# Attention with a top-1 expert mixture on one core: a mask in another pool, two reordered steps, one PSUM bank and new order edges at the changeover

## The chip, the core and the metric

The kernel runs on one core of one Trainium2 chip. The metric is the device time of one execution in microseconds (us); three executions of the kernel before lie between 932.32 and 932.95 us, their median is 932.58 us.

## The reference, cut to what matters

```python
# attention: B=8 batches, H=8 heads, S=576 positions, D=64
scores = q @ k^T / 8 + min(-(cum_i - cum_j), 0)      # cum = cumsum(max(s, 0)); above the diagonal: -1e9
attn   = softmax(scores); x = (attn @ v) as 4608 tokens of 512 values
# mixture: 4 groups of 4 experts, one expert for each token
g_logits = x @ w_group;     g = argmax;  g_w = softmax(g_logits)[g]
e_logits = x @ w_expert[g]; e = argmax;  e_w = softmax(e_logits)[e]
out[token] = g_w * e_w * (relu(x @ w1[g, e]) @ w2[g, e])     # w1: 512 x 1024, w2: 1024 x 512
```

## The kernel before, in words

**Two stages.** Attention runs head by head (64 steps, two heads are a pair `p`), and the mixture runs expert by expert (16 "slots", the fullest expert first). Every product is made of two or three matmuls on high and low parts of its operands, so that each float32 operand is first cast (ScalarE, `wh`, `xh`, `hh`) and its rest is formed by a subtraction (GpSimd or VectorE, `wl`, `xl`, `hl`).

**The order in attention.** `ORDERS` and `FIRST` (L484 to L493) are strings that say in which order the pieces of a step are issued on TensorE, VectorE, ScalarE and GpSimd; these engines work in just this order. `A0` to `A5` are matmuls of a head's row maxima into two PSUM banks `pm` (A1: 64 columns, A2: 192, A3: 320, A4: 448, A5: the second 288), `a` is the maximum that VectorE takes over the oldest of them (`most`, `mx`), `W` is a transpose of `st` on VectorE, `B` and `C` are the scores and the products with V, and `R` runs the next piece of the router. A matmul `A` needs a `pm` bank that an `a` has read. Score tiles, transposes and the router's logits take their banks from `ring`, three banks `ps`; the router's later sums share one bank `pt` (`kept`).

**The router.** For each batch of 576 tokens `Router.batch` is a generator that `R` steps on. Its pieces, in order: the logits (`logits`, L683: 512 columns and the last 64, copied to `lT` by ScalarE), the transposes `pr` of the last 64 rows, the turning matmuls `plt` (L765) with the maximum `lmx` over them (L774), the one-hot choice (`hot`), the counts `pc` (L802), the places in the lists, `rows` and `val`, the list sums `pi` and `pw` (L862), and the weights (`weights`, `finish`; ScalarE's copy `c3p`, L899, ahead of three products `val`, of which the first runs on GpSimd for all batches but the last, L906).

**The changeover.** From step 62 on only TensorE keeps a written order; the other engines' instructions are ordered by a planner that runs the program in its own model and takes what is ready there. The first slot's work is traced after the attention, and `behind(tc, later, earlier)` adds an edge to the order alone: `later` stands behind `earlier`. The first slot has 256 rows of the fullest expert as its `h_items` (96 matmuls `ph`, list `made`, L1383) and `y_items` (64 of `first`, then 32 of `last`, matmuls `py`), and a `rest` tile of 128 more rows, whose token list needs the last batch's list sums. Expert 0's weights come in four loads of 1 MB (`raw`, L1000): two for w1, two for w2; each is cast in four pieces (`wts[0].casts[0]` to `[15]`, L1002, ScalarE) and has four subtractions (`wl`, L1005, GpSimd). The first `py` needs casts from `[8]` on, the `last` matmuls need `wl`.

**Memory.** The pools of attention lie one behind the other in SBUF: `raw` (27648 bytes of each partition), `wa` (77824), `big` (22528), `sm` (15808), `late`, `end`. Those of the mixture use the same bytes again from the same start: `x1` (28672), `wp` (65536), `hp` (24576), `x2` (26624: `xg1`, the third load `raw`, `xh`, `xl`), `wq`, `sp`. A tile waits for the tiles whose bytes it takes.

Of the kernel before, what the change touches and what calls it, by code (L numbers as in the profile page):

```python
# [8 lines left out]
F32 = mybir.dt.float32  # L9
# [3 lines left out]
AF = mybir.ActivationFunctionType  # L13
# [6 lines left out]
B, H, S, D = 8, 8, 576, 64  # L20
P = 128
# [84 lines left out]
def behind(tc, later, earlier):  # L106

    tc.add_manual_dep(later.ins, earlier.ins.name, mybir.DependencyInfo(mybir.DependencyClass.NoSync,
                                                                       mybir.DependencyReason.DATA), reason="behind")


def attention(tc, qk, v, s, wr, xs, st):
    nc = tc.nc
    NP = B * H // 2
    LEAD = 4
    with ExitStack() as ctx:
# [4 lines left out]
        sm = ctx.enter_context(tc.tile_pool(name="sm", bufs=2))  # L121
        late = ctx.enter_context(tc.tile_pool(name="late", bufs=1))
        end = ctx.enter_context(tc.tile_pool(name="end", bufs=1))
        ac = late
# [318 lines left out]
        ones(2)  # L443
        ones(1)

        mask = ac.tile([P, S], F32, name="mask")
        nc.gpsimd.memset(mask, 0.0)
        nc.gpsimd.affine_select(out=mask[:, S - P:], in_=mask[:, S - P:], pattern=[[-1, P]],
                                compare_op=ALU.is_ge, fill=-8.0e9, base=0, channel_multiplier=1)
# [24 lines left out]
        def store_sums():  # L474
# [7 lines left out]
        vals, sums, pts = {}, {}, {}  # L482

        ORDERS = [o.split() for i, o in enumerate((  # L484
# [16 lines left out]
        for step in [-4, -3] + list(range(NH + 5)):  # L501
            m, a = step + LEAD, step - 1
# [109 lines left out]
class Router:  # L612
# [70 lines left out]
    def logits(self, b, x):  # L683

        nc, lT = self.tc.nc, self.lT
        out = []
        for a, e in ((0, 512), (512, S)):
            ps = self.ps_s(f"lg{b}_{a}")
            for c in range(4):
                i = nc.tensor.matmul(ps[32 * c:32 * c + 32, 0:e - a], self.wr_f[:, c], x[:, c, a:e], start=True, stop=True)  # L690
            out.append((lT[:, a:e], ps[:, 0:e - a]))
        for o, ps in out:
            nc.scalar.copy(o, ps)  # L693
        self.st.logged = i
# [37 lines left out]
    def batch(self, b, x):  # L732
        tc, sm, st = self.tc, self.sm, self.st
        nc = tc.nc
# [15 lines left out]
        ps = self.ps_s(f"pr{b}")  # L750
# [12 lines left out]
        ps = self.ps_t(f"plt{b}")  # L763
        for t in range(NB):
            st.turned = nc.tensor.matmul(ps[:, t * 20:(t + 1) * 20], lT[:, t * P:(t + 1) * P], self.sum4,  # L765
                                         start=(t == 0), stop=(t == NB - 1))
        G = [P, NB * 5, 4]

        def quads(c):
# [8 lines left out]
        df = T("df", G[1:])  # L778
        V.tensor_tensor(out=df, in0=lgv, in1=mb, op=ALU.subtract)
        ex = df  # L780
# [67 lines left out]
        C4 = [P, NB, E * NL]  # L848
# [21 lines left out]

        def weights(bank):
            if b != B - 2:
                nc.scalar.activation(ex, df, AF.Exp)
                yield 1
            wf = bank[:, 128:128 + NB * 5]
            w = wf.rearrange("p (t g) -> p t g", g=5)
            cwp, rem = bank[:, 160:160 + NB], bank[:, 168:168 + NB]
            c3p = bank[:, 176:176 + 3 * NB].rearrange("p (j t) -> p j t", t=NB)
            with after(tc, st.routed):
                summed = V.tensor_reduce(out=wf, in_=ex, axis=AX.X, op=ALU.add)  # L880
            if b == B - 2:
                st.put_off.append(summed)
            V.tensor_scalar(out=wf, in0=wf, scalar1=1e-9, scalar2=None, op0=ALU.add)
            V.reciprocal(wf, wf)
            yield
            ws = T("ws", [NB, 4])
            V.tensor_tensor(out=ws, in0=w[:, :, 1:5], in1=oh[:, :, 0], op=ALU.mult)
            wsum = T("wsum", [NB])
            V.tensor_reduce(out=wsum, in_=ws, axis=AX.X, op=ALU.add)
            for x in (cwp, st.cw[:, b]):  # L890
                V.tensor_tensor(out=x, in0=wsum, in1=w[:, :, 0], op=ALU.mult)
            yield

            c3 = T("c3", [3, NB], BF16)
            V.tensor_copy(c3[:, 0], cwp)
            V.tensor_tensor(out=rem, in0=cwp, in1=c3[:, 0], op=ALU.subtract)
            V.tensor_copy(c3[:, 1], rem)
            V.tensor_tensor(out=c3[:, 2], in0=rem, in1=c3[:, 1], op=ALU.subtract)
            nc.scalar.copy(c3p, c3)  # L899
            return c3, c3p  # L900

        def finish(c3, c3p):
            for j in range(3):
                yield
                with after(tc, st.routed):
                    if b < B - 1 and j == 0:  # L906
                        nc.gpsimd.tensor_tensor(out=val[:, 2 + j], in0=colf, in1=c3[:, j].unsqueeze(2).to_broadcast(C4),
                                                op=ALU.mult)
                    else:
                        st.valued = V.tensor_tensor(out=val[:, 2 + j], in0=colf,  # L910
                                                    in1=c3p[:, j].unsqueeze(2).to_broadcast(C4), op=ALU.mult)
            yield 2
            listed(2, 5, "pw")
# [22 lines left out]
def moe(tc, w1, w2, xs, st, out):  # L936
    nc = tc.nc
    V = nc.vector
    ident, mc = st.ident, st.cst
    with ExitStack() as ctx:  # L940
# [93 lines left out]
        class Slot:  # L1034


            def __init__(self, u, w, cap, xg, ids, cw):
                self.u, self.w, self.cap, self.xg, self.ids, self.cw = u, w, cap, xg, ids, cw
                self.rows = [min(P, cap - t) for t in range(0, cap, P)]
                self.products, self.turns, self.highs = [], [], []  # L1040

            def gather(self):
                for t, r in enumerate(self.rows):
# [40 lines left out]
            def h_items(self):  # L1084
                u, cap = self.u, self.cap
                self.hh = hp.tile([P, 8, 384], F32R, name=f"hh{u}", tag="hh")
                self.hl = hp.tile([P, 8, 384], F32R, name=f"hl{u}", tag="hl")

                pss = {}

                def first(f):

                    pss[f] = acc(f"ph{u}_{f}")
                    half(f, 0)
                    half(f, 2)

                def half(f, c0):
                    for c in (c0, c0 + 1):
                        for x in (self.xh, self.xl):
                            product(f, self.w.h, x, c)  # L1100

                def opening():
                    for f in range(4):
                        pss[f] = acc(f"ph{u}_{f}")
                    for c in (0, 2):
                        for f in (1, 2, 0, 3):
                            half(f, c)

                def last(f):
                    for c in range(4):  # L1110
                        product(f, self.w.l, self.xh, c)
                    relu(f)

                def relu(f):
                    ps, hh = pss.pop(f), self.hh[:, f, :cap]
                    self.rounded = nc.scalar.activation(hh, ps[:, :cap], AF.Relu)  # L1116
                    V.scalar_tensor_tensor(out=self.hl[:, f, :cap], in0=ps[:, :cap], scalar=0.0,  # L1117
                                           in1=hh.bitcast(F32), op0=ALU.max, op1=ALU.subtract)

                def product(f, w, x, c, stop=None):  # L1120
                    self.products.append(nc.tensor.matmul(pss[f][:, :cap], w[f // 4][:, c, (f % 4) * P:(f % 4 + 1) * P], x[:, c, :cap],  # L1121
                                     start=(c == 0 and w is self.w.h and x is self.xh),
                                     stop=(c == 3 and w is self.w.l) if stop is None else stop))

                def item(f):
                    if f == 0:

                        pss[f] = acc(f"ph{u}_{f}")
                        for c0 in (0, 2):
                            for w in (self.w.h, self.w.l):  # L1130
                                for c in (c0, c0 + 1):
                                    product(f, w, self.xh, c, False)
                        for c in range(4):
                            product(f, self.w.h, self.xl, c, c == 3)
                        relu(f)
                        return
                    first(f)
                    last(f)

                if u == 0:  # L1140

                    return [opening] + [lambda f=f, part=part: part(f) for part, h in ((last, 0), (first, 4), (last, 4))
                                        for f in range(h, h + 4)]
                return [lambda f=f: item(f) for f in range(8)]
# [169 lines left out]
        wts = [Expert(0, st.e0[0:1, 0:1]), Expert(1, st.e0[0:1, 1:2])]  # L1314
# [56 lines left out]
        with tc.manual_schedule(engines={ENG.PE}):  # L1371
# [10 lines left out]
            run(h)  # L1382
            made = first.products  # L1383
            behind(tc, made[34], st.logged)
            behind(tc, made[45], st.turned)
            behind(tc, made[63], st.counted)
            Y, R = first.y_items(), rest.items()
            del made[:]
            run(Y[:5])
            behind(tc, made[3], st.listed[0])  # L1390
            behind(tc, st.listed[2], made[-4])
            run(Y[5:6])
            run(R[:1])
# [269 lines left out]
```

## Time and profile before

| | |
|---|---|
| median of three executions | 932.58 us |
| the profiled execution, its span | 931.89 us, 930.1 us |
| TensorE busy (share of the span) | 870.8 us (94%) |
| VectorE, ScalarE, GpSimd busy | 690.0, 609.7, 620.1 us (74%, 66%, 67%) |
| mean granted TensorE clock | 0.974 of 2.4 GHz |

The profile is one execution. A line of the timeline has the start in us, the busy time in us, the engine, the source line, the operation, what it writes and reads, how many instructions are merged in the line, and in brackets how long the engine sat idle just before and whose result ended that. PE is TensorE, DVE VectorE, ACT ScalarE, POOL GpSimd, SP the queue that issues the loads. PEclk is the granted TensorE clock (1.00 is 2.4 GHz, 0.50 is 1.2 GHz).

### The profile page before, as it was taken

Reading aid. Unit: us, or ns where it says so; the run is one execution under the profiler, and the core shown is the slowest. Engines: PE = TensorE matmul, PEld = TensorE weight load, DVE = VectorE, ACT = ScalarE, POOL = GpSimd, SP = SyncE. Lnnn points to the kernel's source line nnn. Section 1 sums busy time; section 2 is a strip of 40 time slices with the busy share of each in tenths; the row PEclk is TensorE's granted clock in tenths of the full one; section 3 lists DMA queues with packets and bytes.
Section 4 is the critical chain, followed back from the end, with each engine's and each line's share of the span. In section 5 each row is a group of like instructions: output and inputs, shape, how many; then the busy total and the mean of one; then the engine's idle time right before and its main releaser. Section 6 shows DMA issues by size and latency. Waiting matters only on the chain. (4 is left out here: it accounts for less than half of the span.)

```text
span 930.1 us, 17673 instructions
## 1 busy us (share of the span) xinstructions
PE 870.8 (94%) x5689; PEld 788.6 (85%) x5689; DVE 690.0 (74%) x1986; ACT 609.7 (66%) x1310; POOL 620.1 (67%) x732
## 2 busy tenths in 40 slices
PE   4999999999999999999879999999999999999993
PEld 3788787888878787887768999999999999999992
DVE  7677585858768585885548578898888898888830
ACT  3688686777767777766537467657676666766740
POOL 8798475666757575643467756666777778878750
PEclk9999999999999999999879999999999999999997
DMA  7776565465546555423525645446554556655510
GB/s 151 179 169 177 128 161 141 123 162 144 154 99 161 142 144 139 109 84 138 187 82 194 214 162 198 184 167 227 177 205 170 210 175 226 228 208 196 185 44 23
DMA packets 65004, 148.10 MB, mean 159 GB/s; under 512 B 7588, under 2 KB 40996, under 8 KB 54728
## 3 DMA queue, kind: packets, MB, share of 16 engines
q1 hardware_dynamic: 55020, 126.98, 45.6%
q0 software_dynamic: 7488, 18.89, 5.6%
q10 hardware_dynamic: 2396, 1.02, 0.4%
q8 instruction: 47, 0.77, 0.4%
q14 instruction: 53, 0.43, 0.2%
HBM read 108.97 MB, written 19.69 MB: 138 GB/s over the span
## 5 line engine op out<-in xcount | busy, mean ns | idle before, releaser
L1005 POOL TENSOR_TENSOR wl<-raw,wh 128x512 fp32r<-128x512 f32 x182 | 232.3, 1297 | 47.8 <-ACT wh L1002 34.7
L159 POOL TENSOR_TENSOR WB<-r,WA 64x576 fp32r<-64x576 f32 x128 | 181.5, 1418 | 32.9 <-PE pm L208 7.1
L216 DVE CUSTOM_DVE_ANT_0 mx<-pm,mask 128x192 bf16<-128x192 f32 (+4 forms) x320 | 128.9, 418 | 44.4 <-PE pm L208 41.7
L1002 ACT CAST wh<-raw 128x512 fp32r<-128x512 f32 x256 | 153.9, 617 | 0.4 <-POOL wl L1005 0.4
L208 PE MATMUL pm<-WA 66*128 66x288 f32 (+4 forms) x384 | 129.6, 363 | 22.0 <-DVE mc L216 10.5
L1121 PE MATMUL ph<-xh,wh 128*128 128x256 f32 (+13 forms) x512 | 142.7, 305 | 2.6 <-ACT xh L1078 1.9
L1121 PE MATMUL ph<-xl,wh 128*128 128x256 f32 (+13 forms) x512 | 139.7, 304 | 0.3
L265 PE MATMUL ps<-WA 68*128 68x320 f32 (+4 forms) x384 | 136.7, 360 | 3.2 <-ACT lT L693 2.2
L284 POOL TENSOR_SCALAR_AFFINE_SELECT pt<-pt 128x128 f32<-128x128 f32 (+2 forms) x192 | 64.1, 338 | 96.8 <-ACT pt L275 92.3
L1191 PE MATMUL py<-hh,wh 128*128 128x256 f32 (+13 forms) x448 | 116.0, 307 | 6.3 <-ACT wh L1002 6.3
L305 PE MATMUL po<-pt,VT 128*128 128x256 f32 (+3 forms) x512 | 120.4, 355 | 0.4 <-issue 0.3
L1191 PE MATMUL py<-hl,wh 128*128 128x256 f32 (+13 forms) x448 | 117.1, 308 | 2.3 <-DVE hl L1117 2.0
L267 PE MATMUL ps<-WB 128*128 128x320 f32 (+4 forms) x384 | 111.4, 303 | 0.0
L305 PE MATMUL po<-pu,VT 128*128 128x320 f32 (+1 forms) x384 | 108.6, 391 | 0.0
L1237 DVE STREAM_TRANSPOSE yr<-yT 32x384 f32<-32x384 f32 (+1 forms) x208 | 104.5, 502 | 4.3
L1074 DVE STREAM_TRANSPOSE xt<-xg 32x256 f32<-32x256 f32 (+1 forms) x208 | 102.5, 493 | 3.2
L305 PEld LDWEIGHTS po<-pt,VT 128*128 128x128 f32 x512 | 89.1, 194 | 14.7 <-issue 1.3
L208 PEld LDWEIGHTS pm<-WA 66*128 66x128 f32 (+1 forms) x384 | 70.8, 194 | 35.9 <-DVE mc L216 18.6
L1121 PEld LDWEIGHTS ph<-xh,wh 128*128 128x128 f32 x512 | 96.1, 191 | 5.9 <-ACT xh L1078 3.6
L1121 PEld LDWEIGHTS ph<-xl,wh 128*128 128x128 f32 x512 | 95.8, 191 | 1.8 <-DVE xl L1079 1.2
L1116 ACT ACTIVATE hh<-ph 128x256 fp32r<-128x256 f32 (+13 forms) x128 | 53.9, 422 | 65.2 <-PE ph L1121 64.4
L275 ACT ACTIVATE pt<-ps 128x256 f32<-128x256 f32 (+2 forms) x192 | 76.5, 399 | 25.7 <-PE ps L267 12.1
(243 smaller groups left out, 1840.7 us busy)
## 6 DMA issues: line engine op xcount, KB each, us to landing
raw<-in_w_dram SPq DMA_DIRECT2D x64, 1024.0 KB
WB<-WA SPq DMA_DIRECT2D x64, 288.0 KB
r<-in_qk_dram SPq DMA_DIRECT2D x31, 576.0 KB
VT<-in_v_dram SPq DMA_DIRECT2D x32, 384.0 KB
xs<-xr SPq DMA_DIRECT2D x15, 512.0 KB
xs<-xrt SPq DMA_DIRECT2D x7, 128.0 KB
xg<-xs,ids POOLq DMA_INDIRECT x46
out_dram<-yr,ids POOLq DMA_INDIRECT x43
```

The lines of the kernel that those rows point to most:

```text
L159: i = nc.gpsimd.tensor_tensor(out=wb[64 * a:64 * a + 64, a, h], in0=r[:, h, a], in1=w[0:64, a, h, QO:].bitcast(F32), op=ALU.subtract)
L208: nc.tensor.matmul(ps[:rows, :cw], WA[i][0:66, QA, h, QO + q0:QO + q0 + rows], WA[i][0:66, KA, h, QO + c0:QO + c0 + cw], start=True, stop= ...
L216: nc.vector.tensor_tensor_reduce(out=tmp[:rows, :cw], in0=ps[:rows, :cw], in1=mk[:rows], scale=1.0, scalar=-3.0e38 if c0 == 0 else mo, op0 ...
L265: nc.tensor.matmul(ps[:rows, o:o + w], WA[i][0:68, KA, h, QO + k0:QO + k0 + rows], WA[i][0:68, QA, h, QO + q0:QO + q0 + w], start=True, st ...
L267: nc.tensor.matmul(ps[:rows, o:o + w], WB[p % NBB][:, KA, h, k0:k0 + rows], WB[p % NBB][:, QA, h, q0:q0 + w], start=False, stop=True)
L305: i = nc.tensor.matmul(po[0][:, qa - base:qb - base], VT[p % NVT].rearrange("p t a d -> p (t a d)")[:, (3 * t + 1 + h) * 64:][:, 0:P], x[: ...
L1002: self.casts.append(nc.scalar.copy(h[:, j], raw[:, j]))
L1005: self.low = nc.gpsimd.tensor_tensor(out=l[:, j], in0=raw[:, j], in1=h[:, j].bitcast(F32), op=ALU.subtract)
L1074: V.transpose(dst[:, 0:n, :, j], src[:, 0:n, :, i])
L1121: self.products.append(nc.tensor.matmul(pss[f][:, :cap], w[f // 4][:, c, (f % 4) * P:(f % 4 + 1) * P], x[:, c, :cap], start=(c == 0 and w ...
L1191: self.products.append(nc.tensor.matmul(pss[c][:, :cap], w[2 + f // 4][:, f % 4, c * P:(c + 1) * P], x[:, f, :cap], start=(f == 0 and w is ...
L1237: V.transpose(dst[:, 0:n, :, i], src[:, 0:n, :, j])
```

## The change

The causal mask, 2304 bytes of each partition, is made in pool `sm` and not in `late`. In the string for even steps the last `a R a` becomes `a a R`. The last 64 columns of the logits take the bank `pt` in all batches but the last. The first of three `val` products goes to VectorE in batch 6 too. At the changeover the order edges are others: the last batch's turning matmuls stand exactly between the 55th and the 56th `ph` matmul, its counts ahead of the 78th (the 64th before), its first list sum ahead of the ninth `py` (the fourth before); and on ScalarE the exponential of the last batch stands behind cast 11, the copy `c3p` of the last batch and the ReLUs of the last four `ph` tiles behind cast 15.

```diff
-        mask = ac.tile([P, S], F32, name="mask")
+        mask = sm.tile([P, S], F32, name="mask", tag="mask", bufs=1)
...
-            "b S R B0 Q R v b a A0 B2 v C0 e G a R a B3 T C1 A3 B1 A2 C2 b e t R C3 v G C4 B4 J b D v e a R a A1 "
+            "b S R B0 Q R v b a A0 B2 v C0 e G a R a B3 T C1 A3 B1 A2 C2 b e t R C3 v G C4 B4 J b D v e a a R A1 "
             "W e A4 C5 e C6 b a A5",
...
-            ps = self.ps_s(f"lg{b}_{a}")
+            ps = (self.ps_t if a and b < B - 1 else self.ps_s)(f"lg{b}_{a}")
...
+            st.turning = st.turned if t == 0 else st.turning
...
-                nc.scalar.activation(ex, df, AF.Exp)
+                st.powers = nc.scalar.activation(ex, df, AF.Exp)
...
-            nc.scalar.copy(c3p, c3)
+            st.thirds = nc.scalar.copy(c3p, c3)
...
-                    if b < B - 1 and j == 0:
+                    if b < B - 2 and j == 0:
...
+                    self.rounds.append(self.rounded)
...
-            behind(tc, made[45], st.turned)
-            behind(tc, made[63], st.counted)
+            behind(tc, st.turning, made[54])
+            behind(tc, made[55], st.turned)
+            behind(tc, made[77], st.counted)
+            behind(tc, st.powers, wts[0].casts[11])
+            for i in [st.thirds] + first.rounds[4:]:
+                behind(tc, i, wts[0].casts[15])
             Y, R = first.y_items(), rest.items()
             del made[:]
             run(Y[:5])
-            behind(tc, made[3], st.listed[0])
+            behind(tc, made[8], st.listed[0])
```

## Rows read from the trace of the kernel before

**Rows 1.** Three stretches of 20 us: busy time of PE, PEld, DVE, ACT, POOL, then PEclk.
```profile
260.00:280.00 20.00, 18.52 (x110) 15.46 (x110) 14.86 (x60) 12.44 (x27) 10.45 (x16) 0.91 0.36 88
460.00:480.00 20.00, 13.69 (x84) 13.04 (x85) 12.62 (x51) 7.20 (x17) 7.03 (x7) 0.67 0.20 63
540.00:560.00 20.00, 20.00 (x129) 20.00 (x128) 17.30 (x32) 11.73 (x24) 9.78 (x9) 1.00 0.42 141
```
**Rows 2.** Timeline of TensorE at the changeover.
```profile
456.68 0.68 PE L862 MATMUL pw<-val,rows 128*128 128x192 bf16 x5 [1.81 <-POOL val L907]
457.89 2.05 PE L765 MATMUL plt<-sum,lT 128*128 128x20 f32 x10 [0.54 <-DVE lists L868]
...
466.88 2.08 PE L1121 MATMUL ph<-xh,wl 128*128 128x256 f32 x16
...
475.67 0.58 PE L1191 MATMUL py<-hh,wh 128*128 128x256 f32 x1 [6.31 <-ACT wh L1002]
...
489.62 0.60 PE L1265 MATMUL prr_x<-ident,xg 128*128 128x128 f32 x4
```
**Rows 3.** Timeline of ScalarE at the changeover.
```profile
460.80 0.38 ACT L1116 ACTIVATE hh<-ph 128x256 fp32r<-128x256 f32 x1 [5.44 <-PE ph L1121]
...
474.90 0.17 ACT L899 CAST pk<-c 128x15 f32<-128x15 bf16 x1 [5.51 <-DVE c L898]
475.00 6.33 ACT L1002 CAST wh<-raw 128x512 fp32r<-128x512 f32 x12
```
**Rows 4.** Timeline of GpSimd at the changeover.
```profile
455.91 0.71 POOL L907 TENSOR_TENSOR val<-col,c 128x320 bf16<-128x320 bf16 x1
472.05 1.03 POOL L574 DMA_INDIRECT xg<-xs,ids  x1 [15.43 <-DVE pk L605]
473.10 1.39 POOL L1309 MEMSET xg<- 128x1536 f32 x1
...
478.41 13.73 POOL L1005 TENSOR_TENSOR wl<-raw,wh 128x512 fp32r<-128x512 f32 x11
```
**Rows 5.** Timeline of the load queue: third and fourth load of expert 0.
```profile
445.74 0.34 SPq L1000 DMA_DIRECT2D raw<-in_w_dram  x1
...
450.52 0.33 SPq L1000 DMA_DIRECT2D raw<-in_w_dram  x1
```
**Rows 6.** One microsecond, columns as in Rows 1, last DMA share and GB/s.
```profile
457.00:458.00 1.00, 0.46 (x6) 0.23 (x3) 0.35 (x1) 0.00 (x0) 0.00 (x0) 1.00 0.51 74
```
**Rows 7.** Timeline of VectorE in the last batch's router.
```profile
459.98 0.26 DVE L774 TENSOR_REDUCE lmx<-plt 128x25 f32<-128x100 f32 x1 [2.23 <-PE plt L765]
...
464.68 0.25 DVE L819 TENSOR_TENSOR pc<-pc,count 128x80 f32<-128x80 f32 x1 [2.38 <-PE pc L802]
...
467.72 0.88 DVE L855 TENSOR_TENSOR val<-col,pk 128x320 bf16<-128x320 bf16 x2
```
**Rows 8.** Timeline of VectorE around three of the logit maxima in attention.
```profile
155.67 0.26 DVE L774 TENSOR_REDUCE lmx<-plt 128x25 f32<-128x100 f32 x1 [2.08 <-PE plt L765]
...
209.84 0.27 DVE L774 TENSOR_REDUCE lmx<-plt 128x25 f32<-128x100 f32 x1 [2.08 <-PE plt L765]
...
210.31 0.35 DVE L216 CUSTOM_DVE_ANT_0 mx<-pm,mask 128x192 bf16<-128x192 f32 x1
...
211.28 0.18 DVE L216 CUSTOM_DVE_ANT_0 mx<-pm,mask 64x64 bf16<-64x64 f32 x1
...
262.26 0.26 DVE L774 TENSOR_REDUCE lmx<-plt 128x25 f32<-128x100 f32 x1 [2.08 <-PE plt L765]
```
**Rows 9.** Timeline of TensorE after the second of them.
```profile
210.73 0.47 PE L208 MATMUL pm<-WA 66*128 66x448 f32 x1 [0.86 <-DVE mc L216]
...
211.87 0.53 PE L208 MATMUL pm<-WA 66*128 66x288 f32 x1
...
223.40 0.47 PE L208 MATMUL pm<-WA 66*128 66x448 f32 x1 [0.51 <-DVE mc L216]
```
**Rows 10.** Who waited for L693, the copies of the logits: us, times.
```profile
  PE ps L265: 2.2, 7
```

More of the change, by code (lines that the diff above doesn't have):

```diff
@@ L1039, in __init__ @@
                 self.rows = [min(P, cap - t) for t in range(0, cap, P)]
-                self.products, self.turns, self.highs = [], [], []
+                self.products, self.turns, self.highs, self.rounds = [], [], [], []
             def gather(self):
```

## The prediction, made before the change was run

> **What bounds the kernel now.** I read the stretches of 20 us first. In the mixture TensorE is busy for 20.00 of 20 us at the full clock, so nothing but fewer or earlier matmuls helps there. Two places differ: the changeover, with 13.69 us busy and a clock of 0.67, and once in each batch of the attention a stretch like 260 to 280, with 18.52 us and 0.91 [rows 1]. So the end is set by TensorE, and the change can gain where TensorE idles or runs at 1.2 GHz.
>
> Second view, TensorE's timeline at the changeover: three gaps, 1.81 us for GpSimd's product of batch 6, 0.54 us for the list sum, and 6.31 us until the first weight cast of w2 [rows 2]. ScalarE's timeline gives the reason for the last: the casts start at 475.00, right behind the copy of the last batch, for which ScalarE had waited 5.51 us; from 455.4 to 460.80 it was idle as well [rows 3]. Were the weights late? No: the loads were issued at 445.74 and 450.52 [rows 5], and in the microsecond from 457 on the DMA has fallen to 74 GB/s [rows 6], so both had landed by about 457. The casts stood in the wrong place in ScalarE's order. GpSimd does the same: 15.43 us idle ahead of the rest tile's gather, and the subtractions only from 478.41 [rows 4].
>
> Third view, VectorE and TensorE around one logit maximum. VectorE waits 2.08 us for the turning matmuls, then takes `lmx`, then the maximum over 192 columns [rows 8]. TensorE's 448-column matmul needs the bank that this reads, and idles 0.86 us [rows 9]. The same stall, 0.85 or 0.86 us, stands in six batches (0 to 5). The clock falls to 0.50 some microseconds after five of the six; after the one at 210.73 it does not.
>
> **The change, part by part.**
>
> *Maximum ahead of the router (`a a R`).* The 192-column maximum is then done before VectorE waits, and the 448-column matmul may start at 210.73 - 0.86 = 209.87. The next one, 288 columns, followed it by 1.14 us [rows 9], so at 211.01; but it needs the 64-column maximum, which stays behind `lmx` and the transpose and moves up only by the 0.3 us that the 192 columns took: from 211.28 to 211.0, with its 0.18 us to 211.2 or 211.3 [rows 8]. So a wait of about 0.3 us is new. Per batch 0.86 - 0.3 = 0.55, six times 3.3 us. Bounds: 0 if VectorE's order only moves the wait, 6 x 0.86 = 5.2 if none is left. In the other even steps this `R` has other pieces; one of them has the 0.51 us wait at 223.40 [rows 9], which would also turn into one at the 288 columns. I count nothing for it (bounds 0 and 6 x 0.5).
>
> *The clock behind it.* From maximum to maximum is a period of one batch: 209.84 - 155.67 = 54.17 us with a drop, 262.26 - 209.84 = 52.42 us without [rows 8]. So one drop costs 1.75 us, five 8.75. A gap of 0.51 us had no drop behind it [rows 9], and a gap of 0.3 us would be left. I take four of five as gone: 7.0 us. Bounds: none gone, and the sixth batch drops too (-1.75), to all gone (8.75).
>
> The Trainium skill (TensorE: Matmul & The Clock Gate, "What's actually happening") has the half rate as the default state, which activity releases, watched without regard to where the kernel is. That agrees with equal gaps of 0.86 us with and without a drop; by it a shorter gap may still meet one, and this is rival C.
>
> *Tail of the logits in the other bank.* Score matmuls waited seven times, 2.2 us in all, for the copies that free the logits' banks [rows 10]. With one bank less taken from the ring the next score tile finds a free one. The bank `pt` had its last use, the list sum of the batch before, long ago, and its next use, the turning, comes behind the same copies anyway. I take 1.8 us; bounds 0 and 2.2.
>
> *Product of batch 6 on VectorE.* It costs VectorE 0.44 us (two such took 0.88 [rows 7]) where its work is off TensorE's path, and saves the 1.81 us for GpSimd, which came to it only at 455.91, behind eight subtractions [rows 4]. If that cover failed, the 0.44 us would shift the turning by as much.
>
> *Mask in `sm`.* By the sizes, `x2` ends 145408 bytes behind the start of `raw` and `late` began at 143808: the two overlap by 1600 bytes. With the mask in `sm`, `late` begins at 146112 and they don't. The real load did not wait for this (445.74), but the planner's order looks as if it thought so: a memset of `xg1`, which needs nothing of the last batch, stands behind the gather at 473.10 [rows 4], as do all casts and subtractions of w2. I expect it now to place the loads, the casts and the subtractions early. The mask's two instructions at the start stay as they are.
>
> *Casts first.* Eight casts of 6.33 / 12 = 0.53 us [rows 3] fit into ScalarE's idle time from 455.4 on: the third load's at once, the fourth's from 457, all done by about 461. Queued behind them are the exponential, the last copy and four ReLUs, which now have to wait for the fourth load; the matmuls ahead of the first of those ReLUs end around 462 (454.87 + 0.68 + 0.68 for the list sum and the counts, 1.0 for the turning, 39 x 0.13; worked out below), so this costs nothing. Six of the eight subtractions, 13.73 / 11 = 1.25 us each [rows 4], fit before the gather, the last two are held behind it by an old edge.
>
> *Order edges of the last batch.* The turning moves behind ten more matmuls, the counts behind 22 matmuls after it, the first list sum behind 27 more. A matmul takes 2.08 / 16 = 0.13 us [rows 2]: 2.9 us cover the first chain on VectorE, 464.68 - 2.38 - 459.98 = 2.3 us; 3.5 us do not quite cover the second, 468.60 - 464.68 = 3.9 us [rows 7].
>
> *Sum of the changeover.* From the end of the last busy matmul, 456.68 - 1.81 = 454.87, to the rest tile's transposes at 489.62 are 34.75 us [rows 2]. In it lie 51 `ph` and 80 `py` matmuls, 131 x 0.13 = 17.0 us at the full clock; the turning, half of 2.05 at the full clock, 1.0 (an estimate); four groups of counts and list sums, each taken like `pw` at 0.68, 2.7. With 1.5 us of waits left (0.4 for the second chain, the rest for subtractions `hl` and the last list sum) this is 22.2 us: a gain of 12.5. Bounds: 4 (rival B) and 15 (no wait left, a little less for a matmul). From there everything follows TensorE, whose mixture has no idle time to absorb the shift.
>
> *Total:* 3.3 + 7.0 + 1.8 + 12.5 = 24.6 us off the profiled execution's 931.89 (span 930.1 and 1.8 around it): 907.3. The median was 0.7 above that execution: **908 us**.
>
> **The rivals.**
>
> *B, GpSimd holds the subtractions behind the gathers still.* For: it idled 15 us for them before [rows 4], and no edge forbids it. Against: the moved mask. The counts end around 461.4, the second chain with 3.9 us at 465.3 and not at 468.60, so the gathers come 3 to 4 us earlier and still take 6.4 us (472.05 to 478.41), the eight subtractions follow, and the `last` matmuls wait for them: a gain of 4 us and not 12.5. Time 908 + 8.5 = 916.5.
>
> *C, the drops stay.* For: one equal gap had none, so the gap's length is not all. Then the 7.0 us go and a sixth batch may pay 1.75: 908 + 8.75 = 917.
>
> *D, the weights become the bound.* Expert 1's loads wait for the subtractions of expert 0, then for casts of their own; if slot 1 has to wait for them, part of the changeover's gain comes back, say 8 to 12 of 12.5: 918. Against: these subtractions move up as far as the matmuls do.
>
> *E, slower: ScalarE blocked behind the fourth load.* Four ReLUs and the copy now cannot pass casts 12 to 15. If the planner puts the fourth load behind the gather (issued 472 and not 450.52), it lands 6.5 us later, at 478.5, the casts end at 480.6, and the ninth `py`, which needs the fifth ReLU, runs at about 481.3 instead of 477.8 (475.67 and eight matmuls at half the clock, 0.26 each, an estimate): 3.5 us lost, and if attention gains nothing, 936. It decides from an issue after about 468.5. Against: the load needs only the first load's buffer, free at 450.5.
>
> **How the numbers follow.** Forecast 0.56, with its own range 902 to 913; B 0.14, C 0.17, D 0.07, E 0.06. The lower end 902 is all upper bounds without the last microsecond or so (931.89 + 0.7 - 5.2 - 8.75 - 2.2 - 15 = 901.4); the upper end 921 takes in B, C and D alone and leaves E and two of them together outside. A difference under 0.2% (1.9 us) counts as no change. Faster 0.92, same 0.02 (two rivals together with a low attention gain), slower 0.06.
>
> **What would show it.** Right: the first w2 cast on ScalarE near 456 and not 475; no 6.31 us gap before the first `py`; the rest tile's transposes 12 us closer to the `pw` of batch 6; 448-column matmuls behind the turning without a wait and a 0.3 us one at 288 columns; periods near 52 us. Wrong: subtractions still behind the gathers (B), stretches at 0.50 once a batch (C), new waits for `wh` or `wl` in slot 1 (D), ScalarE idle ahead of cast 12 (E).

## The result and the profile after

The changed kernel takes 906.76 us (median; 906.09 to 908.10 in 4 executions) against 932.45 (932.05 to 932.95) for the kernel before on the same chip: a ratio of 0.9726, 95% interval 0.9709 to 0.9743. The forecast was 908. The profiled execution took 906.31 us with a span of 904.6 and a granted clock of 0.993 over the whole of it; before these were 931.89, 930.1 and 0.974. The difference of the two profiled executions is 25.58 us.

Where it came from is read at three marks on TensorE: the first `ph` matmul of the first slot (called the end of attention here), the rest tile's transposes `prr_x` (end of the changeover), and the first `ph` of expert slot 1, 128x368.

| mark | before | after | earlier by |
|---|---|---|---|
| first `ph` | 446.23 | 432.59 | 13.64 |
| `prr_x` | 489.62 | 463.14 | 26.48 |
| slot 1's first `ph` | 498.65 | 472.23 | 26.42 |
| end of the span | 930.1 | 904.6 | 25.5 |

So attention gave 13.64 us, the changeover another 12.84. Nothing was gained behind it, and 0.9 us was given back: slot 1's matmuls now wait once for a new releaser, `yrr` on VectorE, 0.73 us, and one matmul `py` at 702.93 waits 0.33 us for `hl`; the trace of before has neither. Line numbers are one to three higher than before (L1191 is now L1193). Stretches of 20 us, columns as in [rows 1]: us, busy time of PE, PEld, DVE, ACT, POOL with counts, PEclk, DMA share, GB/s.
```profile
260.00:280.00 20.00, 19.82 (x130) 16.67 (x129) 17.15 (x75) 15.79 (x35) 13.72 (x22) 1.00 0.63 163
440.00:460.00 20.00, 18.10 (x157) 17.28 (x156) 16.03 (x67) 9.50 (x24) 16.29 (x14) 1.00 0.54 178
460.00:480.00 20.00, 19.32 (x124) 16.93 (x123) 16.16 (x40) 14.23 (x31) 13.71 (x13) 1.00 0.59 212
540.00:560.00 20.00, 20.00 (x134) 20.00 (x133) 17.44 (x34) 13.78 (x28) 12.40 (x11) 1.00 0.53 189
```
The stretch with 18.52 us busy at 0.91 is now 19.82 at 1.00, the one with 13.69 at 0.67 is 19.32 at 1.00, and the mixture (last row) is full as it was. These are the same times and not the same work, which now comes 6 to 26 us earlier. For the same work, from the first `ph` to slot 1's first `ph`, TensorE was busy for 43.25 of 52.42 us at a mean clock of 0.84 before, and for 36.91 of 39.64 us at 1.00 after: of the 12.78 us, 6.34 are busy time, the same matmuls at the full clock, and 6.44 are idle time. TensorE's timeline at the changeover, answering to [rows 2]; columns are start, us, engine, line, operation, tiles, count, and in brackets the idle time before and its releaser:
```profile
441.43 0.69 PE L863 MATMUL pw<-val,rows 128*128 128x192 bf16 x5
442.99 1.19 PE L765 MATMUL plt<-sum,lT 128*128 128x20 f32 x10
...
447.85 2.08 PE L1123 MATMUL ph<-xh,wl 128*128 128x256 f32 x16
449.77 0.28 PE L1193 MATMUL py<-hh,wh 128*128 128x256 f32 x1
452.79 0.56 PE L863 MATMUL pi<-val,rows 128*128 128x128 bf16 x5 [1.90 <-DVE val L856]
...
463.14 0.66 PE L1267 MATMUL prr_x<-ident,xg 128*128 128x128 f32 x4 [0.45 <-DVE lists L869]
```
The waits of 1.81, 0.54 and 6.31 us are gone; one of 1.90 us is new, for the second chain's products on VectorE, and one of 0.45 ahead of the transposes is new too. Their reason is in ScalarE's and GpSimd's timelines, answering to [rows 3, 4]:
```profile
442.34 4.26 ACT L1003 CAST wh<-raw 128x512 fp32r<-128x512 f32 x8 [0.32 <-ACT hh L1117]
446.51 0.28 ACT L874 ACTIVATE df<-df 128x100 f32<-128x100 f32 x1
448.53 1.82 ACT L1117 ACTIVATE hh<-ph 128x256 fp32r<-128x256 f32 x4 [1.74 <-PE ph L1123]
458.45 0.17 ACT L900 CAST pk<-c 128x15 f32<-128x15 bf16 x1 [8.10 <-DVE c L899]
```
```profile
441.05 1.38 POOL L1311 MEMSET xg<- 128x1536 f32 x1
442.39 10.01 POOL L1006 TENSOR_TENSOR wl<-raw,wh 128x512 fp32r<-128x512 f32 x8
455.61 1.02 POOL L574 DMA_INDIRECT xg<-xs,ids  x1 [3.21 <-DVE pk L605]
456.66 1.30 POOL L1006 TENSOR_TENSOR wl<-raw,wh 128x512 fp32r<-128x512 f32 x1
```
The eight casts stand ahead of the exponential (`df`) and the wait for the last copy, not behind them; the memset stands ahead of the gather, for which GpSimd idles 3.21 us and not 15.43, and so do seven of w2's eight subtractions (the first of the `x8` at 442.39 still belongs to w1: w2's first cast has only begun at 442.34). The eighth follows the gather, at 456.66. Expert 0's third and fourth load, the two of w2, were issued as much earlier as attention ended earlier and no more ([rows 5] less 13.64), by the load queue's timeline:
```profile
432.10 0.34 SPq L1001 DMA_DIRECT2D raw<-in_w_dram  x1
...
436.89 0.33 SPq L1001 DMA_DIRECT2D raw<-in_w_dram  x1
```
VectorE around a logit maximum and TensorE behind it, answering to [rows 8, 9]:
```profile
100.10 0.27 DVE L775 TENSOR_REDUCE lmx<-plt 128x25 f32<-128x100 f32 x1 [1.80 <-PE plt L765]
...
201.81 0.34 DVE L216 CUSTOM_DVE_ANT_0 mx<-pm,mask 128x192 bf16<-128x192 f32 x1
203.96 0.27 DVE L775 TENSOR_REDUCE lmx<-plt 128x25 f32<-128x100 f32 x1 [1.80 <-PE plt L765]
204.50 0.77 DVE L344 STREAM_TRANSPOSE st<-rc 128x576 f32<-128x576 f32 x1
205.20 0.17 DVE L216 CUSTOM_DVE_ANT_0 mx<-pm,mask 64x64 bf16<-64x64 f32 x1
```
```profile
203.77 0.51 PE L208 MATMUL pm<-WA 66*64 66x64 f32 x2
204.11 1.24 PE L305 MATMUL po<-pu,VT 128*128 128x320 f32 x4
205.52 0.40 PE L208 MATMUL pm<-WA 66*128 66x288 f32 x1 [0.17 <-DVE mc L216]
```
The 192-column maximum is taken 2.2 us before `lmx`; the 448-column matmul, recorded here as the second of the `x2` at 203.77, has no wait, and 0.17 us is left at the 288 columns. A period of one batch is (203.96 - 100.10) / 2 = 51.93 us in the first two, and 51.71 to 51.84 us in the next three. No stretch of attention or changeover is at half clock any more; before, five of the six batches had one behind the turning, there was one from 34 to 39 us, and two in the changeover (458 to 465, 471 to 482). One microsecond of such a stretch before, columns as in [rows 6]:
```profile
158.00:159.00 1.00, 1.00 (x5) 0.80 (x3) 1.00 (x4) 0.42 (x1) 0.64 (x1) 0.50 0.97 207
```

### The profile page after: what moved, and what is told of

The parts are those of the page before. It is cut to its first block, busy times and chain, and to the rows that moved or that the text cites. A ratio compares the mean times of both kernels' runs of the same rounds, so it can differ in the third digit from the quotient of the medians.

```text
span 904.6 us, 17681 instructions
## 1 busy us (share of the span) xinstructions
PE 858.3 (95%) x5689; PEld 774.3 (86%) x5689; DVE 689.9 (76%) x1987; ACT 610.3 (67%) x1310; POOL 619.2 (68%) x731
## 5 line engine op out<-in xcount | busy, mean ns | idle before, releaser
L208 PE MATMUL pm<-WA 66*128 66x288 f32 (+4 forms) x384 | 123.8, 353 | 16.1 <-DMA WA<-ch 9.7
L265 PE MATMUL ps<-WA 68*128 68x320 f32 (+4 forms) x384 | 133.9, 352 | 1.0 <-ACT pu L275 0.9
L1193 PE MATMUL py<-hl,wh 128*128 128x256 f32 (+13 forms) x448 | 115.0, 304 | 2.5 <-DVE hl L1119 2.2
L1193 PE MATMUL py<-hh,wh 128*128 128x256 f32 (+13 forms) x448 | 113.0, 302 | 0.0
L305 PE MATMUL po<-pu,VT 128*128 128x320 f32 (+1 forms) x384 | 105.2, 382 | 0.0
L208 PEld LDWEIGHTS pm<-WA 66*128 66x128 f32 (+1 forms) x384 | 68.1, 190 | 36.8 <-DVE mc L216 21.6
L1123 PE MATMUL ph<-xh,wl 128*128 128x256 f32 (+13 forms) x512 | 92.5, 299 | 0.0
```

The source lines that it names most:

```text
L208: nc.tensor.matmul(ps[:rows, :cw], WA[i][0:66, QA, h, QO + q0:QO + q0 + rows], WA[i][0:66, KA, h, QO + c0:QO + c0 + cw], start=True, stop= ...
L265: nc.tensor.matmul(ps[:rows, o:o + w], WA[i][0:68, KA, h, QO + k0:QO + k0 + rows], WA[i][0:68, QA, h, QO + q0:QO + q0 + w], start=True, st ...
L305: i = nc.tensor.matmul(po[0][:, qa - base:qb - base], VT[p % NVT].rearrange("p t a d -> p (t a d)")[:, (3 * t + 1 + h) * 64:][:, 0:P], x[: ...
L1193: self.products.append(nc.tensor.matmul(pss[c][:, :cap], w[2 + f // 4][:, f % 4, c * P:(c + 1) * P], x[:, f, :cap], start=(f == 0 and w is ...
```

## The experiments

The kernel before does not repeat exactly: its medians beside the three groups of experiments were 926.37, 928.07 and 929.65 us, and single executions ran from 925.04 to 932.70. Each experiment is therefore read by its ratio to the kernel before on its own chip, and by the marks of its profile. The marks of before are those of its one profile, an execution of 931.89 us; "between" runs from the first `ph` to slot 1's first `ph`:

| kernel | median us | ratio [95%] | first `ph` | slot 1's `ph` | between |
|---|---|---|---|---|---|
| before | 932.45 | 1 | 446.23 | 498.65 | 52.42 |
| after | 906.76 | 0.9726 [0.9709, 0.9743] | 432.59 | 472.23 | 39.64 |
| e1_order | 918.76 | 0.9895 [0.9849, 0.9942] | 434.42 | 485.73 | 51.31 |
| e2_bank | 924.63 | 0.9971 [0.9945, 0.9997] | 440.06 | 490.18 | 50.12 |
| e3_both | 917.55 | 0.9882 [0.9835, 0.9929] | 433.10 | 484.35 | 51.25 |
| e4_mask | 922.47 | 0.9937 [0.9916, 0.9958] | 446.12 | 490.69 | 44.57 |
| e6_nomask | 915.06 | 0.9866 [0.9841, 0.9891] | 431.86 | 481.49 | 49.63 |
| e8_pool | 913.15 | 0.9844 [0.9820, 0.9868] | 432.77 | 479.43 | 46.66 |
| e11_pins | 904.71 | 0.9768 [0.9735, 0.9800] | 431.69 | 470.50 | 38.81 |
| e7_nocasts | 906.73 | 0.9759 [0.9731, 0.9788] | 431.86 | 472.99 | 41.13 |
| e9_pi24 | 904.57 | 0.9739 [0.9711, 0.9768] | 431.98 | 470.79 | 38.81 |
| e12_pi22 | 905.01 | 0.9743 [0.9715, 0.9772] | 432.51 | 471.26 | 38.75 |

### Attention: the order, the bank, and the clock

**e1_order** is the kernel before with `a a R` alone.
```
-... J b D v e a R a A1 "
+... J b D v e a a R A1 "
```


> The kernel before with the order `a a R` alone. Theory (the 0.86 us wait makes the clock fall): the wait moves to the 288-column matmul and shrinks to about 0.2 us, and the stretches at 0.50 go in all batches: 6 x 0.6 + 5 x 1.75 = 12 us, about 920. Rival (the turning matmuls themselves, with 20 columns each, make it fall): the stretches at 0.50 stay and only the waits go, about 929.

Measured: 918.76 us. Attention ends 446.23 - 434.42 = 11.81 us earlier than in the profile of before, and has no stretch at half clock; the changeover keeps its stalls, as TensorE's timeline shows:
```profile
462.74 0.58 PE L1191 MATMUL py<-hh,wh 128*128 128x256 f32 x1 [6.46 <-ACT wh L1002]
```
By the medians on its own chip, 926.37 and 918.76 us, the order is worth 7.6 us and not 11.8: most executions of the kernel before were faster there than the profiled one. In its profile the order alone leaves no drop behind the turnings, and with that goes most of attention's gain. Its four executions lie within 1.1 us, the thirteen of the kernel before beside them within 7.3. The stretch from 34 to 39 us is gone too, but e10, which has the old order, does not have it either.

**e2_bank** is the kernel before with the tail of the logits in the router's bank alone.
```
-            ps = self.ps_s(f"lg{b}_{a}")
+            ps = (self.ps_t if a and b < B - 1 else self.ps_s)(f"lg{b}_{a}")
```


> The kernel before with the logits' tail in the router's bank alone. Theory: the seven waits for the logits' copies go (2.2 us), the 0.86 us waits and the stretches at 0.50 stay: about 930.5. Rival (this edit, not the order, removed the low clock in attention): 920 to 923.

Measured: 924.63 us, 0.3% better, with an interval that almost reaches 1. Its profile has the half-clock stretch behind three of six turnings (102 to 106, 208 to 212, 314 to 318) and the one at 34, where the kernel before had five of six in one execution. The gap at the turning stays, 0.92 or 0.93 us in all six batches where before had 0.85 or 0.86, so the same gap comes with and without a drop. The 6.17 us by which its attention ends earlier than before hold two drops less beside the bank's own worth.

**e3_both** has both edits. 

> The kernel before with both attention edits and nothing at the changeover. Theory: the changed kernel's first matmul of the first slot came 13.6 us earlier than before, and all of it is due to these two, so about 919, with the 6.31 us gap at the changeover as before. Rival (the two overlap, or the changeover gives some of it back): 921 to 925.

Measured: 917.55 us, and attention ends at 433.10, 1.32 us earlier than in e1. Neither of the two has a drop in attention, so this is the bank's worth: 1.32 us, or 1.99 us counted from the first `lmx` (99.82 in e1, 100.49 in e3). It is 1.2 us by the medians, though the runs of the two overlap (917.09 to 918.75 and 918.32 to 919.44).

**e10_rows2** asks whether a gap as such lowers the clock. In the kernel before, VectorE makes the comparison `rows` twice, so that the 448-column matmul of the odd step, which has no turning matmuls ahead of it, waits longer. The result of the kernel is the same.
```
+        V.tensor_tensor(out=rows, in0=self.cols.unsqueeze(1).to_broadcast([P, NB, P]),
+                        in1=pl.unsqueeze(2).to_broadcast([P, NB, P]), op=ALU.is_equal)
```


> The kernel before, with the 0.80 us comparison that makes `rows` done twice in each batch, which lengthens the wait of the 448-column matmul two steps after the turning from 0.5 to about 1.3 us, with no turning matmuls near it. Theory (the gap alone makes the clock fall): six new stretches at 0.50, 6 x (0.8 + 1.75) = 15 us, about 948. Rival (it takes the turning matmuls with the gap): no new stretches, 6 x 0.8 = 5 us, about 937.

Measured: 933.47 and 934.20 us. Two further executions took 1074 and 1805 us at a mean granted clock of 0.75 and 0.488; why is not known, and there is no ratio. The question is answered by its profile, by TensorE's timeline at both kinds of gap:
```profile
155.20 0.47 PE L208 MATMUL pm<-WA 66*128 66x448 f32 x1 [0.85 <-DVE mc L216]
...
170.39 0.47 PE L208 MATMUL pm<-WA 66*128 66x448 f32 x1 [1.37 <-DVE mc L216]
...
225.50 0.47 PE L208 MATMUL pm<-WA 66*128 66x448 f32 x1 [1.39 <-DVE mc L216]
```
and the stretches right behind them (columns as above):
```profile
155.00:160.00 5.00, 4.80 (x17) 3.84 (x18) 3.21 (x11) 1.33 (x4) 1.40 (x1) 0.66 0.61 136
...
170.00:174.00 4.00, 3.61 (x21) 3.13 (x22) 3.78 (x15) 2.54 (x6) 2.04 (x3) 1.00 0.38 81
225.00:229.00 4.00, 3.50 (x21) 3.01 (x21) 3.78 (x14) 2.51 (x6) 1.93 (x3) 1.00 0.35 74
```
The longer gap of 1.23 to 1.39 us stands in six batches (at 115, 170, 225, 278, 333 and 388 us) and the clock stays at 1.00 behind all six. Behind the turning, where the gap is 0.85 us and ten matmuls of 20 columns come ahead of it, the clock falls in four of six. So the length of a gap alone does not decide, and the theory is refuted. In attention a drop behind a turning came only where the gap stood behind it (e1 has the turning without the 0.85 us and no drop), and not always. It is no rule that it takes both: the stretch from 34 to 39 us in before has no turning ahead of it, and neither has one in e7 (below), behind a gap of 1.90 us after matmuls of 256 columns. What decides between two equal places stays open.

### The changeover: mask, casts, the product, the pins

**e4_mask** is the kernel before with the mask in the other pool and nothing else.
```
-        mask = ac.tile([P, S], F32, name="mask")
+        mask = sm.tile([P, S], F32, name="mask", tag="mask", bufs=1)
```


> The kernel before with the mask in the other pool alone. Theory (the planner holds the third load's tile back while its pool shares bytes with `late`): the eight w2 casts go ahead of the fifth ReLU and the subtractions ahead of the rest tile's gather, the 6.31 us gap goes, the waits for GpSimd's product of batch 6 stay or grow: 6 to 9 us, about 925. Rival (the order edges on ScalarE do it, the mask only its place): no change, 932.

Measured: 922.47 us. Attention ends where it did (446.12), the changeover is 52.42 - 44.57 = 7.85 us shorter, though not a single edge of order was changed. ScalarE's and then GpSimd's timeline:
```profile
455.87 4.26 ACT L1002 CAST wh<-raw 128x512 fp32r<-128x512 f32 x8 [0.60 <-ACT xrt L754]
```
```profile
455.92 1.26 POOL L1005 TENSOR_TENSOR wl<-raw,wh 128x512 fp32r<-128x512 f32 x1
457.15 0.71 POOL L907 TENSOR_TENSOR val<-col,c 128x320 bf16<-128x320 bf16 x1
457.82 8.64 POOL L1005 TENSOR_TENSOR wl<-raw,wh 128x512 fp32r<-128x512 f32 x7
473.38 1.04 POOL L574 DMA_INDIRECT xg<-xs,ids  x1 [6.91 <-DVE pk L605]
```
The casts start at 455.87 and not at 475.00, and all subtractions but the last have moved ahead of the gather, by the mask alone; the 6.31 us gap of TensorE is gone, and with it the half-clock stretch from 471 to 482. The two loads of w2 are issued at 445.63 and 450.42, as before: it is the work behind them that moved. In exchange the product of batch 6 comes later on GpSimd, and TensorE waits 3.14 us for it, where 1.81 stood before; the clock is at half for most of 457 to 465, as it was in before from 458 to 465:
```profile
457.91 1.07 PE L862 MATMUL pw<-val,rows 128*128 128x192 bf16 x5 [3.14 <-POOL val L907]
```
```profile
455.00:465.00 10.00, 6.55 (x32) 6.01 (x31) 3.99 (x18) 5.08 (x11) 10.00 (x9) 0.66 0.58 191
```

**e6_nomask** is the changed kernel with the mask back in its old pool and without the two lines of cast edges (the diff of e4 reversed, and that of e7).

> The changed kernel with the mask in the old pool and without the order edges behind the casts. Theory: casts and subtractions go back behind the last copy and the gathers, and the changeover loses 9 to 12 us: about 917. Rival (the other edges, not the mask, brought the changeover's gain): 907 to 909.

Measured: 915.06 us, a changeover of 49.63 us. The casts are back behind the last copy (457.84) and the gap is back on TensorE:
```profile
458.51 0.58 PE L1193 MATMUL py<-hh,wh 128*128 128x256 f32 x1 [5.88 <-ACT wh L1003]
```

**e7_nocasts** is the changed kernel without the cast edges, the mask in its new pool.
```
-            behind(tc, st.powers, wts[0].casts[11])
-            for i in [st.thirds] + first.rounds[4:]:
-                behind(tc, i, wts[0].casts[15])
```


> The changed kernel without the order edges behind the casts (exponential, last copy, four ReLUs). Theory (with the mask moved the planner puts the casts there by itself): 907, no change. Rival (the edges are needed): the casts fall behind the ReLUs or the last copy, 909 to 917.

Measured: 906.73 us (905.61 to 907.64), the same as after. ScalarE and GpSimd go through the same order of work with and without the edges: with the mask moved, the planner places the casts there by itself. Its stage is 41.13 us and not 39.64, since the clock falls for some microseconds behind the 1.90 us wait that after has in the same place without a drop. TensorE's timeline and one microsecond of the stretch:
```profile
452.06 0.56 PE L863 MATMUL pi<-val,rows 128*128 128x128 bf16 x5 [1.90 <-DVE val L856]
453.56 0.41 PE L1193 MATMUL py<-hl,wh 128*128 128x256 f32 x1
```
```profile
454.00:455.00 1.00, 1.00 (x6) 1.00 (x6) 0.85 (x5) 0.00 (x0) 0.12 (x1) 0.50 0.00 0
```
e6 and e7 differ in the mask alone, so the mask is worth 49.63 - 41.13 = 8.5 us of the stage there, 8.3 by the medians, where 9 to 12 were expected; what the edges would do with the mask in its old place was not tried.

**e8_pool** is the changed kernel with the product of batch 6 back on GpSimd.
```
-                    if b < B - 2 and j == 0:
+                    if b < B - 1 and j == 0:
```


> The changed kernel with the product of batch 6 back on GpSimd. Theory: it stands there behind seven subtractions, a memset and one more subtraction, the list sum of batch 6 waits about 3 us for it, and the clock may fall behind that: 909.5 to 912. Rival (the matmuls pinned ahead of the turning cover it): 907.

Measured: 913.15 us, 6.4 more than after and above the range that was expected. In GpSimd's order the product now stands behind the memset and one subtraction; TensorE's and the 4-us view show what that costs:
```profile
444.58 0.68 PE L863 MATMUL pw<-val,rows 128*128 128x192 bf16 x5 [1.96 <-POOL val L908]
```
```profile
444.00:448.00 4.00, 2.88 (x18) 2.59 (x18) 0.84 (x3) 2.80 (x6) 4.00 (x4) 0.81 0.68 236
448.00:452.00 4.00, 4.00 (x21) 4.00 (x19) 1.43 (x7) 0.29 (x1) 4.00 (x5) 0.50 0.39 125
452.00:456.00 4.00, 4.00 (x37) 3.77 (x37) 2.43 (x12) 1.47 (x4) 1.14 (x1) 0.83 0.40 168
```
The wait is 1.96 us (and 0.54 more ahead of the turning), and behind it the matmuls run at half clock: 21 of them in the 4 us from 448, where the stretch behind it at 0.83 has 37. The stage is 7.0 us longer than after (46.66 against 39.64), but not all of it is the product's: the clock falls once more from 460 to 464, behind the 1.90 us wait at `pi` (458.50), where it fell in e7 and did not in after. In e7 that made the stage 41.13 - 39.64 = 1.5 us longer, which leaves some 5.5 us for the product (an estimate).

**e11_pins** is the changed kernel with the old places of the router's matmuls in TensorE's order.
```
-            behind(tc, st.turning, made[54])
-            behind(tc, made[55], st.turned)
-            behind(tc, made[77], st.counted)
+            behind(tc, made[45], st.turned)
+            behind(tc, made[63], st.counted)
...
-            behind(tc, made[8], st.listed[0])
+            behind(tc, made[3], st.listed[0])
```


> The changed kernel with the three old places of the last batch's matmuls among the first slot's (turning, counts, first list sum). Theory (the new places only fit the order, the gain is in the casts): within 1 us of 907. Rival (without the matmuls ahead of it, the turning waits for the list sum of batch 6, and the first list sum stalls ahead of the fourth `py`): 909 to 911.

Measured: 904.71 us (903.72 to 908.59), lower than either expected; the changeover is 38.81 us, 0.8 shorter than after, with waits of 0.54, 0.18 and 0.45 us and none ahead of `pi`. So the new places are not needed for the gain. With the old ones 36 matmuls stand between the counts and the first list sum, with the new ones 27.

**e9_pi24** and **e12_pi22** move the first list sum behind more of the `py` matmuls, to take away the new 1.90 us wait; e12 also puts the counts three matmuls earlier.
```
-            behind(tc, made[8], st.listed[0])
+            behind(tc, made[24], st.listed[0])
```
```
-            behind(tc, made[77], st.counted)
+            behind(tc, made[74], st.counted)
...
-            behind(tc, made[8], st.listed[0])
+            behind(tc, made[22], st.listed[0])
```


> The changed kernel with the first list sum of the last batch ahead of the 25th `py` and not the ninth. Theory: the 1.90 us wait ahead of it is filled with 16 matmuls, and TensorE carries the gain to the end: about 905. Rival (the rest tile's gather or the weights of slot 1 take the time back): 906.5.

> The changed kernel with the counts ahead of the 75th `ph` (78th) and the first list sum ahead of the 23rd `py` (ninth). Theory: VectorE had the one-hot choice 0.4 us before the counts ran, so the chain to the list sum moves up by up to 0.4 us and the 1.90 us wait is filled: about 904.6. Rival: the later wait of the list sum of the weights takes it back, 905 to 906.5.

Measured: 904.57 us (903.69 to 905.81) and 905.01 (904.43 to 906.12), beside 906.73 for e7 on the same chip. The wait ahead of `pi` is gone in both; a wait of 0.65 us for `xlr` on VectorE, at the rest tile's first matmuls `pur`, comes in its place, and in e9 the one at `prr_x` is 0.60 and not 0.45. From 440 to 460 TensorE of e9 has no idle time:
```profile
440.00:460.00 20.00, 20.00 (x173) 19.01 (x171) 15.41 (x65) 9.50 (x23) 16.15 (x14) 1.00 0.54 180
```
e9 is the version that I would keep. It is ahead of the kernel before (ratio 0.9739) and of e7, which does the same work as the changed kernel, by about 2 us, with runs that overlap by 0.2 us; part of the 2 us may be the drop behind the wait that e9 does not have. Between e9, e11 and e12 no difference is measured.

## Why the prediction was right, and which terms were off

The place, the direction and the main mechanisms were right: the drops behind the turnings, the casts and subtractions held back by the mask's place. That 908 was only 1.2 us from the median is in part luck: the sum of 24.6 us (25.58 measured) holds errors that cancel. The size of the gain also depends on the execution of the kernel before: the profiled one lies at the slow end, and on another chip e7, which does the same work as the changed kernel, is 22.9 us ahead of it (929.65 and 906.73).

*Maximum ahead of the router.* Right in kind: no wait at the 448 columns, a new one at the 288, 0.17 us where 0.3 was put. Too large in size. The only period without a drop on both sides, from the third maximum to the fourth, went from 52.42 to 255.68 - 203.96 = 51.72 us, and to 52.04 in e1: 0.38 us for the order and 0.32 for the bank, where 0.55 and 0.3 were counted. Over six batches the order is about 2.3 us and not 3.3; the bank is 1.9 by this, 1.3 to 2.0 by e3 against e1, and 1.8 was put. The step that failed is that TensorE would keep what the shorter wait gave: of 0.86 - 0.17 = 0.69 us a part is lost again at once. From the first turning matmul to the next transposes `px` TensorE took 213.63 - 208.53 = 5.10 us before and 207.50 - 202.65 = 4.85 us after.

*The clock.* Too small. No drop is left behind the turnings, where four of five were put. The 1.75 us of one drop compare two different batches. Batch for batch the periods with a drop lost 2.12, 2.25, 2.28 and 2.53 us, the one without 0.70, so a drop was worth 1.4 to 1.8 us and the five about 8. The first `lmx` comes 101.61 - 100.10 = 1.51 us earlier, which the sum did not hold at all. The stretch from 34 to 39 us, which is gone, lies ahead of it; that the change removed it is not shown, since e10, which does the same work up to there as before, lacks it as well, and has its first `lmx` at 100.78. With these terms attention adds up: 2.3 + 1.9 + 8 + 1.5 = 13.7 us, and 13.64 were measured. Rival C (the drops stay) is refuted in after, e1 and e3. That drops come and go with equal gaps, as in e2, agrees with the rule that was set beside it (the Trainium skill, TensorE: Matmul & The Clock Gate, "What's actually happening": the chip looks without regard to where the kernel is). It did not follow that a shorter gap would keep some: none of the profiles with `a a R` has a drop in attention.

*Mask.* Right, and shown: e4 alone moves casts and subtractions and shortens the stage by 7.85 us; without it e6 is 8.5 us longer than e7. The loads were expected early too and did not move against attention's end. Two subtractions were expected to stay behind the gather; one did. Rival B (subtractions behind the gathers) is refuted. That the 1600 bytes of overlap are the cause is argued from sizes; a mask of another size in the old pool was not tried.

*Casts first.* The casts stand where the step put them, but the edges do nothing (e7); the mask does it.

*Product of batch 6.* The step that was misjudged, though it did not show in the total. It was credited with the 1.81 us wait of [rows 2]. Left on GpSimd in the new order it would have cost 5.5 us of the stage and up to 6.4 us in time (e8), since the moved mask puts the memset and a subtraction ahead of it, and the clock falls behind the wait. The mask alone pays such a price inside its 7.85 us: in e4 the wait is 3.14 us.

*Order edges.* Half right. The first chain is covered. The term mis-sized is the 0.4 us for the second chain: it measured 1.90. The chain took from 447.50 to 452.73, 5.2 us instead of 3.9, because four subtractions `hl` of the first slot's last `ph` tiles, 0.42 us each, now stand inside it on VectorE:
```profile
447.50 0.25 DVE L820 TENSOR_TENSOR pc<-pc,count 128x80 f32<-128x80 f32 x1 [1.17 <-PE pc L803]
...
448.94 0.42 DVE L1119 SCALAR_TENSOR_TENSOR hl<-ph,hh 128x256 fp32r<-128x256 f32 x1 [0.29 <-ACT hh L1117]
...
451.85 0.88 DVE L856 TENSOR_TENSOR val<-col,pk 128x320 bf16<-128x320 bf16 x2
```
The price was counted on VectorE's old order, while the same change let ReLUs and their subtractions run earlier. The rest of the sum held it up: from `pw` to the transposes the stage took 463.14 - 441.43 = 21.71 us, with 22.2 worked out from 131 matmuls, the turning (1.19 measured, 1.0 put), four groups and 1.5 us of waits. The new place of the counts also shortened the cover, from 36 matmuls to 27. The old places (e11) would have done as well or better. That the stage gained what was forecast rests on the term that was right: with the 6.31 us gap gone and no half clock left, its matmuls ran at the 0.13 us that was put, or a little less.

*Rivals D and E.* TensorE waits nowhere for `wh` or `wl` in slot 1, so the weights do not bound. The fourth load was issued at 436.89, not behind the gather, and ScalarE finished the eight casts at 446.60, 1.9 us before the next ReLU had its matmuls. Both are refuted. That from the changeover on "everything follows TensorE" was off by the 0.9 us given back there.

## What to carry to other kernels

When loads, casts and fills that need nothing of a late result stand behind it in an engine's order, look for two buffers that share addresses before writing edges of order: here one line of allocation was worth 7.9 to 8.5 us of the stage, and the edges added nothing to it. Then ask of each work that an early-moved block now stands in front of who waits for it: the product left on GpSimd would have taken some 5.5 us of that back. And price a chain with the order that the engine will have after the change, not the one in the trace.

## What the runs showed of the hardware

The granted clock fell behind ten 20-column matmuls followed by 0.85 to 0.93 us of idle time in five (before), three (e2) and four (e10) of six equal places, and in no batch of the profiles with `a a R`, where that idle time is gone. It did not fall behind six gaps of 1.23 to 1.39 us without such matmuls (e10). Behind the same 1.90 us wait it fell in e7 and e8 and not in after. So neither a gap's length nor the narrow matmuls ahead of it tell in these runs whether it falls, and one profile does not show what the next execution does.

Drops that come and go would explain a spread between executions of one program: the kernel before ran from 925.04 to 932.95 us, which is as much as four or five drops of 1.75 us. The granted clocks agree: beside e1 the four fastest executions of the kernel before (925.04 to 925.62 us) have 0.985, the two slowest (932.18 and 932.35) 0.973. Where the half clock lay in them is not shown: of its executions one was profiled.
